# An attention maximum over the partitions, folded on VectorE and spread by two matmuls, in place of ten TensorE transposes

## The chip, the core and the metric

The kernel runs on one core of a Trainium2 chip. Its engines are named as in the profile: PE is TensorE (PEld its weight loads), DVE VectorE, ACT ScalarE, POOL GpSimd, and SP the engine that issues nearly all transfers. The metric is the time of one launch on the device, in microseconds (us); the median of several runs counts. [...]

## What is computed

Attention with queries averaged in pairs, and then a feed-forward layer that takes the largest of three products:

```
q_pool = q.reshape(B, H, S // 2, 2, D).mean(axis=3)          # 8 batches, 8 heads, 576 rows, 64 columns
scores = scale * (q_pool @ k^T)                              # 576 x 1152 a head
scores = scores - max(scores, axis=-1)
attn = exp(scores); attn = attn / (sum(attn, axis=-1) + 1e-9)
x = (attn @ v), heads side by side                           # 4608 x 512
h = max(x @ w1, x @ w2, x @ w3)                              # 4608 x 768
out = h @ w_out                                              # 4608 x 512
```

All is float32 to the outside. Inside, large products are split into a high and a low part in fp32r, a float32 of reduced precision, and summed.

## The kernel before

A **unit** is half the queries (288) of one pair of heads: 8 batches x 4 pairs x 2 halves = 64 units, numbered d = 0 to 63. The keys of a head, 1152, make nine blocks of 128. For each block `kk`, PE computes the scores of both heads transposed, keys on the partitions and 2 x 288 = 576 query columns along the free axis (`pqk`, L538 and L539, four matmuls of 288 columns). ACT copies them to SBUF (`s`, L544), and DVE keeps the running maximum over the blocks (`acc`, 128 x 576, L550 for the first and L553 for the seven others). The nine PSUM results share two buffers: a buffer comes free when its copy and its maximum are done.

After the ninth block `acc` holds, for each query column, 128 candidates, one a partition. The maximum over the partitions is taken in two pieces, of 3 x 115 = 345 columns (h = 0) and of 231 (h = 1). For a piece, PE transposes 116 columns at a time against the identity into PSUM (`pmt`, L589: three transposes, then two), DVE reduces each transposed block along its free axis to one value a query (`m`, L595), and PE transposes the values, broadcast to 128 columns, back over all partitions (`pmb`, L605: three, then two). These are the ten transposes of a unit. DVE then subtracts `pmb` from the scores (L620, three blocks by one piece at a time: 3 x 345 or 3 x 231 columns), ACT takes the exponential (L626), POOL sums over the nine blocks (`ksum`, L639 and L641, one addition of 576 columns each), and PE multiplies by the values (`pav`, L669, 36 matmuls in float32). The row sums go through PE (`psum`), a reciprocal on DVE (`rs`, L690; a column form of 96 x 6 in the first 16 units) and a scaling on POOL or DVE.

Beside that, the feed-forward runs in chunks of mostly 512 tokens, one batch behind the attention: `ph` (L931), `hm` (L952), `po` (L986). In the first third, DVE, ACT and POOL also unpack the feed-forward weights from 64-bit words (`w`, L831 to L864).

The order of all this is set when the program is built. Each piece of work is a `Step` with its engines, an assumed cost, the steps it comes after, and an urgency: the unit's number plus an entry of `RANK` for its kind, plus one of `NUDGE` for its name. `arrange` takes, at each turn, the engine that is free first, and gives it the most urgent step that is ready; where a step names two engines, the first that takes it has it. The result is a fixed list for each engine, and each engine then works through its list strictly in order and waits at the head for what an entry needs. Three dependences matter here. The first maximum of a unit (`kk == 1`) overwrites `acc`, which has one buffer, and so waits for the transposes of the unit before (`old.rows`). The PSUM pools `ps_a` and `ps_b` have one bank each, and hold `pmt`, `pmb` and, in `ps_b` from unit 8 on, `pav`, one after the other. And `pmb` of a unit may be written only after the subtractions of the unit before.

Of the kernel before, what the change touches and what calls it, by code (L numbers as in the profile page):

```python
# [18 lines left out]
P = 128  # L19
# [3 lines left out]
QH = 288  # L23
CB = 115
# [12 lines left out]
    "qk": -94.8622,  # L37
    "cp": -198.877,
    "mx": -110.1936,
    "rows": -297.5399,  # L40
    "red": -97.7108,
    "bc": -69.2978,
    "sub": 36.0255,
    "exp": -154.9623,
    "keys": -14.5562,
    "av": 14.8431,
    "xcopy": -242.7422,
    "psum": 306.6745,
    "eps": 163.4791,
    "inv": 411.5164,  # L50
    "xm": -165.8669,
    "load": 11.9358,
    "prep": 513.6605,
    "move": 372.9744,
    "split": 31.5471,
    "ffn": -33.8173,
    "rate": 1.0394,
    "mm": 49.1178,
    "fetch": -156.7626,
    "evac": -234.7904,  # L60
    "hhigh": 172.1589,
    "hlow": -152.0307,
    "conv": 478.2091,
    "rate0": 4.4379,
    "first_qk": 87.3127,
    "first_cp": -260.4178,
    "first_mx": 25.0784,
    "first_sub": 35.563,
    "first_exp": 326.0935,
    "first_keys": -44.827,  # L70
    "first_av": 37.0199,
    "first_xcopy": -183.8483,
    "first_psum": -32.0782,
    "first_inv": -61.85,
    "first_xm": -117.3451,
    "first_load": -320.6766,
    "first_prep": -184.3904,
    "first_move": -506.8185,
    "first_split": 49.1161,
# [991 lines left out]
```

## Time and profile before

| | |
|---|---|
| median of 3 runs | 1482.36 us (1482.32 to 1483.36) |
| span of the profiled execution, first to last instruction | 1480.9 us |
| TensorE clock granted, mean | 0.975 |
| PE busy with `ph`, `pav`, `pqk`, `po` on the chain that ended last | 27%, 13%, 14%, 10% of the span |
| PE busy with `pmt` and `pmb` on that chain | 2% and 2% |

The page gives no time for the profiled execution but its span. A busy time is the time in which an engine had an instruction at work; matmuls are pipelined, so their durations overlap, and PE's pace is read from one start to the next. "A <- B" in a list of waits says that A sat idle until B was done, with the sum in us, how often, and the longest. Groups of instructions are given as line, engine, operation, output <- inputs, shapes and count, then busy time and mean ns of one, and the idle time before them.

### The profile page before, as it was taken

Reading aid. Unit: us, or ns where it says so; the run is one execution under the profiler, and the core shown is the slowest. Engines: PE = TensorE matmul, PEld = TensorE weight load, DVE = VectorE, ACT = ScalarE, POOL = GpSimd, SP = SyncE. Lnnn points to the kernel's source line nnn. Section 1 sums busy time; section 2 is a strip of 40 time slices with the busy share of each in tenths; the row PEclk is TensorE's granted clock in tenths of the full one; section 3 lists DMA queues with packets and bytes.
Section 4 is the critical chain, followed back from the end, with each engine's and each line's share of the span. In section 5 each row is a group of like instructions: output and inputs, shape, how many; then the busy total and the mean of one; then the engine's idle time right before and its main releaser. Section 6 shows DMA issues by size and latency. Waiting matters only on the chain.

```text
span 1480.9 us, 24740 instructions
## 1 busy us (share of the span) xinstructions
PE 1400.6 (95%) x8704; PEld 1098.3 (74%) x8704; DVE 1046.1 (71%) x1441; ACT 904.5 (61%) x1464; POOL 1078.7 (73%) x835
## 2 busy tenths in 40 slices
PE   4788999888899999999999999999999999999999
PEld 4566666666567878778777777777777777778999
DVE  4898788989896875577777777877777778761110
ACT  4767766647676766467666676676766766651211
POOL 1888977686887868478887898789878988772210
PEclk9989899988999999999999999999999999999999
DMA  6556446657545665465566656664666556424441
GB/s 184 154 160 187 115 132 181 185 176 229 158 120 158 195 190 170 130 196 169 155 184 180 182 142 177 181 190 139 176 180 187 150 165 184 139 72 157 152 159 60
DMA packets 114762, 240.71 MB, mean 163 GB/s; under 512 B 15440, under 2 KB 75216, under 8 KB 114640
## 3 DMA queue, kind: packets, MB, share of 16 engines
q1 hardware_dynamic: 114064, 238.55, 55.2%
q8 instruction: 70, 1.15, 0.3%
q10 hardware_dynamic: 576, 0.59, 0.2%
q14 instruction: 52, 0.43, 0.1%
HBM read 144.70 MB, written 18.87 MB: 110 GB/s over the span
## 4 chain that ended last, share of the span: by engine, by line
PE 70%; DVE 4%; DMA 2%; issue 1%; POOL 1%; ACT 1%; SPq 0%; ACTq 0%; DVEq 0%
PE ph L931 27%; PE pav L669 13%; PE po L986 10%; PE pqk L538 7%; PE pqk L539 7%; PE pmt L589 2%; PE psum L683 2%; PE pmb L605 2%; DVE acc L553 1%; DMA w<-in_wout_dram 1%; DVE s L620 1%; DMA qq<-qraw 1%; POOL ksum L641 0%; DVE w L834 0%; DVE w L839 0%
## 5 line engine op out<-in xcount | busy, mean ns | idle before, releaser
L641 POOL TENSOR_TENSOR ksum<-ksum,s 128x576 f32<-128x576 f32 x448 | 638.0, 1424 | 28.9 <-ACT s L626 5.8
L931 PE MATMUL ph<-xh,w 128*128 128x512 f32 (+2 forms) x1440 | 464.6, 377 | 5.4 <-DVE hm L952 4.0
L620 DVE TENSOR_TENSOR s<-s,pmb 128x1035 f32<-128x1035 f32 (+1 forms) x384 | 396.9, 1049 | 46.0 <-PE pmb L605 46.0
L544 ACT COPY s<-pqk 128x576 f32<-128x576 f32 x576 | 362.5, 638 | 105.2 <-PE pqk L539 101.4
L538 PE MATMUL pqk<-qq,kc 128*128 128x288 f32 x1152 | 360.0, 327 | 57.1 <-DVE acc L553 35.3
L553 DVE TENSOR_TENSOR acc<-acc,pqk 128x576 f32<-128x576 f32 x448 | 335.3, 748 | 84.5 <-ACT s L544 81.7
L626 ACT ACTIVATE s<-s 128x1035 f32<-128x1035 f32 (+1 forms) x384 | 354.8, 934 | 60.2 <-DVE s L620 57.1
L539 PE MATMUL pqk<-qq,kc 128*128 128x288 f32 x1152 | 333.4, 304 | 0.0
L538 PEld LDWEIGHTS pqk<-qq,kc 128*128 128x128 f32 x1152 | 225.5, 196 | 113.5 <-DVE acc L553 51.7
L669 PE MATMUL pav<-s,v 128*64 128x288 f32 x2304 | 306.8, 419 | 1.8 <-DVE xr L724 1.4
L931 PEld LDWEIGHTS ph<-xh,w 128*128 128x128 f32 x1440 | 263.1, 188 | 45.9 <-DVE hm L952 4.9
L931 PE MATMUL ph<-xl,w 128*128 128x512 f32 (+2 forms) x720 | 268.4, 373 | 0.0
L669 PEld LDWEIGHTS pav<-s,v 128*64 128x64 f32 x2304 | 165.1, 141 | 122.0 <-issue 17.7
L539 PEld LDWEIGHTS pqk<-qq,kc 128*128 128x128 f32 x1152 | 227.9, 198 | 11.2
L962 POOL TENSOR_TENSOR h_lo<-hm,h_hi 128x512 fp32r<-128x512 f32 (+2 forms) x60 | 70.8, 1179 | 149.5 <-ACT h_hi L959 149.5
L639 POOL TENSOR_TENSOR ksum<-s 128x576 f32<-128x576 f32 x64 | 91.9, 1436 | 105.5 <-ACT s L626 103.1
L952 DVE TENSOR_TENSOR hm<-hm,ph 128x512 f32<-128x512 f32 (+2 forms) x120 | 75.4, 628 | 127.5 <-PE ph L931 127.5
L931 PEld LDWEIGHTS ph<-xl,w 128*128 128x128 f32 x720 | 135.8, 189 | 11.8
L595 DVE TENSOR_REDUCE m<-pmt 116x3 f32<-116x384 f32 (+1 forms) x128 | 61.1, 488 | 91.9 <-PE pmt L589 91.9
L434 POOL TENSOR_TENSOR kraw<-kraw 128x1152 fp32r<-128x1152 f32 x31 | 82.9, 2675 | 57.1 <-ACT kraw L430 39.4
L690 DVE RECIPROCAL rs<-rs 128x288 f32<-128x288 f32 (+1 forms) x64 | 96.3, 1506 | 18.5 <-ACT rs L687 18.2
L678 ACT COPY xr<-pav 128x288 f32<-128x288 f32 x64 | 25.4, 398 | 114.8 <-PE pav L669 114.6
(57 smaller groups left out, 1288.9 us busy)
## 6 DMA issues: line engine op xcount, KB each, us to landing
w<-w_split SPq DMA_DIRECT2D x144, 512.0 KB, 3.4
kc<-kraw SPq DMA_DIRECT2D x384, 96.0 KB, 2.3
qq<-qraw SPq DMA_DIRECT2D x252, 144.0 KB, 3.1
v<-in_vr_dram SPq DMA_DIRECT2D x32, 576.0 KB, 3.9
kraw<-in_kT_dram SPq DMA_DIRECT2D x31, 576.0 KB, 4.7
qraw<-in_qT_dram SPq DMA_DIRECT2D x31, 576.0 KB, 4.3
w<-in_win_dram SPq DMA_DIRECT2D x18, 512.0 KB, 4.8
w_split<-w SPq DMA_DIRECT2D x18, 512.0 KB, 4.9
```

Of the source, the lines that this page charges most:

```text
L538: nc.tensor.matmul(ps[:, h - hs[0], :QH], w, qq[:, 0, h], start=True, stop=False)
L539: nc.tensor.matmul(ps[:, h - hs[0], :QH], w, qq[:, 1, h], start=False, stop=True)
L544: nc.scalar.copy(o.s[kk // 3][:, kk % 3, slice(*hs)], o.ps[kk, hs][:, :, :QH])
L553: nc.vector.tensor_tensor(acc, acc, ps, op=ALU.max)
L620: nc.vector.tensor_tensor(s, s, o.pb[h][:, None, :w].broadcast_to([P, 3, w]), op=ALU.subtract)
L626: nc.scalar.activation(s, s, AF.Exp, scale=SCALE)
L639: vec[e].tensor_tensor(o.ksum, o.s[0][:, 0], x, op=ALU.add)
L641: vec[e].tensor_tensor(o.ksum, o.ksum, x, op=ALU.add)
L669: nc.tensor.matmul(o.pav[64 * h : 64 * h + 64, :QH], pr.v[:, kk, h], o.s[kk // 3][:, kk % 3, h], start=(kk == 0), stop=(kk == NK - 1),)
L690: nc.vector.reciprocal(o.rs, o.rs)
L931: nc.tensor.matmul(t.ps[:, : hi - lo], w[:, a, kk], xx[:, kk, lo:hi], start=(kk == 0 and i == 0), stop=(kk == 3 and i == 2),)
L986: nc.tensor.matmul(t.ps[:, : hi - lo], ww[:, kk, ms], hh[:, kk, lo:hi], start=(kk == 0 and i == 0), stop=(kk == 5 and i == 2),)
```

## The change

The maximum over the partitions is taken without PE. `fold` is one DVE reduce that reads `acc` in 32 x 32 blocks, transposes each and takes the maximum along the free axis: its result, 128 x 18, holds in each quarter of 32 partitions the maximum over these 32 keys, with query column 32 t + p at partition p, column t. `shift` copies the three upper quarters beside the first (three copies of 32 x 18), and `summit` reduces the four to one (`m`, 32 x 18). `m_high` and `m_low` split that value into an fp32r part and its remainder, on partitions 0 to 31 and 32 to 63 of `ml`. `spread_out` multiplies `ml` with a stacked pair of 32 x 32 identities (`pick`): 64 rows of 576 columns with the values on the diagonals, in one of two buffers `diag0` and `diag1` whose lower half was zeroed once. It may run on DVE or on POOL. Two matmuls of ones (`wide`, 128 x 128) against the halves of `diag`, 288 columns each, then leave the maximum of each column on all 128 partitions (`pmb`).

The pieces are now the two heads, 288 columns each, and subtraction and exponential follow that cut. The first maximum of a unit waits for the fold of the unit before instead of its transposes, and both stand on DVE. `ps_a` and `ps_b` no longer hold `pmt`. The tables `RANK` and `NUDGE` have new entries throughout, so that the order changes everywhere. An SBUF reserve for transfers that POOL would issue (it issues none here) is set to 1024 bytes.

```diff
-CB = 115
+SQ = 32
+NB = 18
...
 RANK = {
-    "qk": -94.8622,
+    "qk": -367.121,
...
 NUDGE = {
-    "av.0": -22.83, "av.1": -51.39, "av.10": -3.73, "av.11": -25.99, "av.12": 22.67, "av.13": 75.61,
+    "av.0": -107.82, "av.1": -655.65, "av.10": 832.07, "av.11": 458.97, "av.12": 42.87, "av.13": -71.19,
...
+    wide = cpool.tile([P, P], F32R, name="wide")
+    nc.vector.memset(wide.bitcast(F32), 1.0)
+    pick = cpool.tile([2 * SQ, SQ], F32, name="pick")
+    for i in range(2):
+        rows = slice(SQ * i, SQ * i + SQ)
+        nc.vector.tensor_copy(pick[rows], ident[rows, rows])
+    diag = [cpool.tile([P, NB, SQ], F32R, name=f"diag{i}") for i in range(2)]
+    for t in diag:
+        nc.vector.memset(t.bitcast(F32), 0.0)
...
-                    after = [c] + ([copies[0]] + (old.rows if old else []) if kk == 1 else [tops[-1]])
+                    after = [c] + ([copies[0]] + ([old.red] if old else []) if kk == 1 else [tops[-1]])
...
-        for h, (x0, x1) in enumerate([(0, 3 * CB), (3 * CB, 2 * QH)]):
-            nb, w = 3 - h, x1 - x0
-
-            def rows(e, h=h, nb=nb, x0=x0):
-                o.pt[h] = pools[h].tile([P, 512], F32, tag="ab"[h], name=f"pmt{d}_{h}")
-                acc = o.acc.rearrange("p h q -> p (h q)")[:, x0:]
-                for i in range(nb):
-                    nc.tensor.transpose(
-                        o.pt[h][: CB + 1, i * P : (i + 1) * P], acc[:, CB * i : CB * i + CB + 1], ident
...
+        def fold(e):
+            o.tops = small.tile([P, 4, NB], F32, tag="tops", name=f"tops{d}")
+            nc.vector.tensor_reduce(
+                o.tops[:, 0],
+                o.acc.rearrange("p h q -> p (h q)").rearrange("p (t k) -> p t k", t=NB),
+                axis=AX.X,
+                op=ALU.max,
+                apply_transpose=True,
+            )
+
+        def shift(e):
+            for g in range(1, 4):
+                nc.vector.tensor_copy(o.tops[:SQ, g], o.tops[SQ * g : SQ * g + SQ, 0])
+
+        def summit(e):
+            o.m = small.tile([SQ, NB], F32, tag="m", name=f"m{d}")
+            nc.vector.tensor_reduce(o.m, o.tops[:SQ].rearrange("p g t -> p t g"), axis=AX.X, op=ALU.max)
+
+        def m_high(e):
+            o.ml = small.tile([2 * SQ, NB], F32R, tag="ml", name=f"ml{d}")
+            nc.vector.tensor_copy(o.ml[:SQ], o.m)
+
+        def m_low(e):
+            nc.vector.tensor_tensor(o.ml[SQ:], o.m, o.ml[:SQ], op=ALU.subtract)
+
+        def spread_out(e):
+            vec[e].tensor_tensor(
+                diag[d % 2][: 2 * SQ],
+                pick[:, None, :].broadcast_to([2 * SQ, NB, SQ]),
+                o.ml[:, :, None].broadcast_to([2 * SQ, NB, SQ]),
+                op=ALU.mult,
+            )
+
+        o.red = step("red", d, [("dve", 0.667)], fold, [tops[-1]])
+        x = step("shift", d, [("dve", 0.24)], shift, [o.red])
+        x = step("top", d, [("dve", 0.142)], summit, [x])
+        y = step("top", d, [("dve", 0.085)], m_high, [x])
+        x = step("top", d, [("dve", 0.085)], m_low, [y])
+        full = step("diag", d, [dve(2 * QH), pool(2 * QH)], spread_out, [x] + (old2.bcs if old2 else []))
+        o.bcs = []
+        for h in range(2):
...
-            x = step("rows", d + 0.1 * h, [pe(133 * nb)], rows, [tops[-1], gone] + (old.subs[h] if old else []))
-            o.rows.append(x)
-            x = step("red", d, [("dve", 0.067 + nb * 0.133)], reduce, [x])
-            b = step("bc", d + 0.1 * h, [pe(89 + 99 * nb)], bcast, [x])
+            b = step("bc", d + 0.1 * h, [pe(133)], bcast, [full, gone] + (old.subs[h] if old else []), cols=QH)
...
-    nc = bacc.Bacc("TRN2", target_bir_lowering=False, num_devices=1)
+    nc = bacc.Bacc("TRN2", target_bir_lowering=False, num_devices=1, dynamic_dma_scratch_size=1024)
```

In the new order the diagonal is made by POOL in 20 units (3, 6, 8, 10, 13, 14, 18, 22, 24, 28, 30, 32, 36, 38, 42, 46, 48, 50, 52 and 59) and by DVE in the other 44. Two places show how the lists changed. A number behind a name's letters is the unit (`acc37` is unit 37's running maximum, `pqk38_0` the first score tile of unit 38, `s37_0` the first three score blocks of unit 37); what follows a last underscore tells buffers apart.

On DVE, at the end of unit 37's running maximum, before the change:

```order
L553 TENSOR_TENSOR acc37_7621<-acc37_7621,pqk37_7_7723 128x576
L690 RECIPROCAL rs35_7738<-rs35_7738 128x288
L553 TENSOR_TENSOR acc37_7621<-acc37_7621,pqk37_8_7733 128x576
L595 TENSOR_REDUCE m37_0_7785<-pmt37_0_7774 116x3
L595 TENSOR_REDUCE m37_1_7797<-pmt37_1_7787 116x2
L620 TENSOR_TENSOR s37_0_7599<-s37_0_7599,pmb37_0_7799 128x3x345
L550 TENSOR_TENSOR acc38_7819<-s38_0_7790,pqk38_1_7792 128x576
```

And at the same place after it:

```order
L578 TENSOR_TENSOR acc37_7444<-acc37_7444,pqk37_8_7564 128x576
L610 TENSOR_REDUCE tops37_7616<-acc37_7444 128x18
L737 RECIPROCAL rs35_7614<-rs35_7614 128x288
L620 COPY tops37_7616<-tops37_7616 32x18 x3
L624 TENSOR_REDUCE m37_7625<-tops37_7616 32x18
L628 CAST ml37_7627<-m37_7625 32x18
L631 TENSOR_TENSOR ml37_7627<-m37_7625,ml37_7627 32x18
L634 TENSOR_TENSOR diag1_109<-pick_105,ml37_7627 64x576
L667 TENSOR_TENSOR s37_0_7408<-s37_0_7408,pmb37_0_7639 128x3x288
L575 TENSOR_TENSOR acc38_7659<-s38_0_7637,pqk38_1_7631 128x576
```

Two reduces that each waited for PE are now a row of eight DVE instructions, with a reciprocal of unit 35 in their midst, and the first subtraction stands behind all of them.

On PE, from the product of unit 36 with its values (`pav36`, of which the last row is shown) to the spread of unit 37's maximum, before the change:

```order
L669 MATMUL pav36_7742<-s36_2_7498,v18_7174 64x288 x6
L589 MATMUL pmt37_0_7774<-ident_94,acc37_7621 116x128 x3
L538 MATMUL pqk38_0_7779<-qq19_0_7531,kc19_0_7425 128x288
L539 MATMUL pqk38_0_7779<-qq19_0_7531,kc19_0_7425 128x288
L538 MATMUL pqk38_0_7779<-qq19_0_7531,kc19_0_7425 128x288
L539 MATMUL pqk38_0_7779<-qq19_0_7531,kc19_0_7425 128x288
L589 MATMUL pmt37_1_7787<-ident_94,acc37_7621 116x128 x2
L538 MATMUL pqk38_1_7792<-qq19_0_7531,kc19_0_7425 128x288
L539 MATMUL pqk38_1_7792<-qq19_0_7531,kc19_0_7425 128x288
L538 MATMUL pqk38_1_7792<-qq19_0_7531,kc19_0_7425 128x288
L539 MATMUL pqk38_1_7792<-qq19_0_7531,kc19_0_7425 128x288
L605 MATMUL pmb37_0_7799<-ident_94,m37_0_7785 128x116 x3
```

And after it:

```order
L716 MATMUL pav36_7594<-s36_2_7353,v18_6964 64x288 x6
L563 MATMUL pqk38_1_7631<-qq19_0_7400,kc19_0_7226 128x288
L564 MATMUL pqk38_1_7631<-qq19_0_7400,kc19_0_7226 128x288
L563 MATMUL pqk38_1_7631<-qq19_0_7400,kc19_0_7226 128x288
L564 MATMUL pqk38_1_7631<-qq19_0_7400,kc19_0_7226 128x288
L652 MATMUL pmb37_0_7639<-diag1_109,wide_103 128x288
L978 MATMUL ph3_2_2_0_7574<-xh_116,w3_8_7453 128x512
L978 MATMUL ph3_2_2_0_7574<-xl_117,w3_8_7453 128x512
L978 MATMUL ph3_2_2_0_7574<-xh_116,w3_8_7453 128x512
L652 MATMUL pmb37_1_7649<-diag1_109,wide_103 128x288
L563 MATMUL pqk38_2_7651<-qq19_0_7400,kc19_0_7226 128x288
```

The transposes are gone, the first score tile of unit 38 now stands ahead of `pav36` (as do three `ph` matmuls behind the last scores of unit 37), and one matmul a piece is left of the spread.

More of the change, by code (lines that the diff above doesn't have):

```diff
@@ L36 @@
 RANK = {
-    "qk": -94.8622,
[L38 to L79, printed above, removed]
+    "qk": -367.121,
+    "cp": -157.85,
+    "mx": -372.477,
+    "red": -424.5991,
+    "shift": 218.3036,
+    "top": 471.3296,
+    "diag": -168.3272,
+    "bc": -652.2135,
+    "sub": 755.1676,
+    "exp": -77.4348,
+    "keys": 484.2481,
+    "av": -155.8274,
+    "xcopy": -495.8442,
+    "psum": 574.5454,
+    "eps": 154.6528,
+    "inv": -26.1003,
+    "xm": -523.4844,
+    "load": -101.8997,
+    "prep": 1286.9188,
+    "move": 398.6518,
+    "split": 200.0963,
+    "ffn": 230.3769,
+    "rate": -0.5905,
+    "mm": 112.971,
+    "fetch": -118.1147,
+    "evac": -754.3044,
+    "hhigh": -198.253,
+    "hlow": -705.5998,
+    "conv": 858.8277,
+    "rate0": 7.3554,
+    "first_qk": -785.226,
+    "first_cp": -585.909,
+    "first_mx": -200.8558,
+    "first_sub": 791.5253,
+    "first_exp": 611.1097,
+    "first_keys": -255.5291,
+    "first_av": -768.3727,
+    "first_xcopy": 8.2676,
+    "first_psum": -145.466,
+    "first_inv": -141.066,
+    "first_xm": 75.1779,
+    "first_load": 150.9309,
+    "first_prep": 256.4223,
+    "first_move": -487.1256,
+    "first_split": 381.6855,
 }
 NUDGE = {
[77 rows of a table removed]
[90 rows of a table added]
 }
@@ L577, in scores @@
                     uses.append([c, x])
-        o.rows, o.subs, o.exps, o.pt, o.pb, o.m = [], [[], []], {}, {}, {}, {}
+        o.subs, o.exps, o.pb = [[], []], {}, {}
         pools = (ps_a, ps_b)
-        for h, (x0, x1) in enumerate([(0, 3 * CB), (3 * CB, 2 * QH)]):
-            nb, w = 3 - h, x1 - x0
-            def rows(e, h=h, nb=nb, x0=x0):
-                o.pt[h] = pools[h].tile([P, 512], F32, tag="ab"[h], name=f"pmt{d}_{h}")
-                acc = o.acc.rearrange("p h q -> p (h q)")[:, x0:]
-                for i in range(nb):
-                    nc.tensor.transpose(
-                        o.pt[h][: CB + 1, i * P : (i + 1) * P], acc[:, CB * i : CB * i + CB + 1], ident
-                    )
-            def reduce(e, h=h, nb=nb):
-                o.m[h] = small.tile([CB + 1, 3], F32, tag=f"m{h}", name=f"m{d}_{h}")
-                nc.vector.tensor_reduce(
-                    o.m[h][:, :nb],
-                    o.pt[h][: CB + 1, : nb * P].rearrange("p (t k) -> p t k", t=nb),
-                    axis=AX.X,
-                    op=ALU.max,
-                )
-            def bcast(e, h=h, nb=nb):
-                o.pb[h] = pools[h].tile([P, 512], F32, tag="ab"[h], name=f"pmb{d}_{h}")
-                for i in range(nb):
-                    nc.tensor.transpose(
-                        o.pb[h][:, CB * i : CB * i + CB + 1],
-                        o.m[h][:, i : i + 1].broadcast_to([CB + 1, P]),
-                        ident[: CB + 1, : CB + 1],
-                    )
-            gone = xout[d - 1] if d > SPLIT and h else None
-            x = step("rows", d + 0.1 * h, [pe(133 * nb)], rows, [tops[-1], gone] + (old.subs[h] if old else []))
-            o.rows.append(x)
-            x = step("red", d, [("dve", 0.067 + nb * 0.133)], reduce, [x])
-            b = step("bc", d + 0.1 * h, [pe(89 + 99 * nb)], bcast, [x])
-            for i in range(3):
-                def sub(e, i=i, h=h, x0=x0, x1=x1, w=w):
-                    s = o.s[i].rearrange("p k h q -> p k (h q)")[:, :, x0:x1]
-                    nc.vector.tensor_tensor(
-                        s, s, o.pb[h][:, None, :w].broadcast_to([P, 3, w]), op=ALU.subtract
-                    )
-                def exp(e, i=i, x0=x0, x1=x1):
-                    s = o.s[i].rearrange("p k h q -> p k (h q)")[:, :, x0:x1]
@@ new lines, in scores, with bcast, sub, exp @@
+        o.red = step("red", d, [("dve", 0.667)], fold, [tops[-1]])
[6 more added lines that the diff above has]
+        for h in range(2):
+            def bcast(e, h=h):
+                o.pb[h] = pools[h].tile([P, 512], F32, tag="ab"[h], name=f"pmb{d}_{h}")
+                nc.tensor.matmul(
+                    o.pb[h][:, :QH],
+                    wide,
+                    diag[d % 2][:, NB // 2 * h : NB // 2 * h + NB // 2].rearrange("p t k -> p (t k)"),
+                    start=True,
+                    stop=True,
+                )
+            gone = xout[d - 1] if d > SPLIT and h else None
+            b = step("bc", d + 0.1 * h, [pe(133)], bcast, [full, gone] + (old.subs[h] if old else []), cols=QH)
+            o.bcs.append(b)
+            for i in range(3):
+                def sub(e, i=i, h=h):
+                    s = o.s[i][:, :, h]
+                    nc.vector.tensor_tensor(
+                        s, s, o.pb[h][:, None, :QH].broadcast_to([P, 3, QH]), op=ALU.subtract
+                    )
+                def exp(e, i=i, h=h):
+                    s = o.s[i][:, :, h]
@@ L626, in exp @@
                     nc.scalar.activation(s, s, AF.Exp, scale=SCALE)
                 r = d + 0.1 * i + 0.05 * h
-                x = step("sub", r, [dve(3 * w)], sub, [b, copies[-1]])
+                x = step("sub", r, [dve(3 * QH)], sub, [b, copies[-1]])
                 o.subs[h].append(x)
-                o.exps[i, h] = step("exp", r, [("act", 0.109 + w / 400)], exp, [x])
+                o.exps[i, h] = step("exp", r, [("act", 0.109 + QH / 400)], exp, [x])
         o.sums = []
```

165 rows, old and new, of the table NUDGE are left out of this document.

## The prediction

> **What bounds the kernel now.** I read the busy times first, then the span in stretches, then who waits for whom in each stretch, and last the order of time around one maximum.
>
> ```profile
> span 1480.9 us, 24740 instructions
> PE 1400.6 (95%) x8704; PEld 1098.3 (74%) x8704; DVE 1046.1 (71%) x1441; ACT 904.5 (61%) x1464; POOL 1078.7 (73%) x835
> ```
>
> ```profile
> 40.00:420.00 380.00, 325.91 (x2133) 237.18 (x2132) 326.42 (x547) 257.98 (x420) 305.11 (x227) 0.91 0.58 167
> 420.00:1327.00 907.00, 903.27 (x5545) 703.61 (x5545) 679.09 (x831) 599.59 (x956) 729.42 (x563) 1.00 0.57 165
> 1327.00:1481.00 154.00, 150.56 (x952) 141.17 (x950) 22.73 (x39) 29.29 (x64) 34.92 (x36) 1.00 0.38 129
> ```
>
> The columns are the length, the busy time of PE, PEld, DVE, ACT and POOL with counts, the granted clock and the DMA share. There are three regimes. From 40 to 420 us PE is busy for 326 of 380 us at a granted clock of 0.91, and DVE for as long: 86% each. From 420 to 1327 us PE is busy for 903 of 907 us at full clock, DVE for 75% and POOL for 80%. The last 154 us are feed-forward matmuls with nothing else beside them. The waits inside the first two stretches (PE's and DVE's for 40 to 420, then the same for 420 to 1327) say which of the two engines leads:
>
> ```profile
> PE pqk L538 <- DVE acc L553: 29.9, 37, 2.9
> DVE acc L553 <- ACT s L544: 22.7, 22, 5.8
> DVE m L595 <- PE pmt L589: 8.1, 11, 1.7
> ...
> PE pmt L589 <- ACT xr L678: 3.0, 4, 0.9
> PE pmb L605 <- DVE m L595: 0.7, 1, 0.7
> DVE m L595 <- PE pmt L589: 82.6, 67, 3.1
> DVE s L620 <- PE pmb L605: 44.9, 40, 3.7
> ```
>
> In the first stretch PE waits 29.9 us for DVE's running maximum: DVE leads. In the second PE waits 3.7 us in all, and DVE waits 127.5 us for the ten transposes (82.6 + 44.9): PE leads, and a microsecond taken from its queue there is a microsecond off the end, if nothing new makes it wait.
>
> **What PE loses and gains.** PE's order of time around the maximum of unit 37 (start, duration, line):
>
> ```profile
> 805.69 0.54 PE L589 MATMUL pmt<-ident,acc 128*116 128x128 f32 x3
> 805.98 0.38 PE L538 MATMUL pqk<-qq,kc 128*128 128x288 f32 x1
> 806.20 0.30 PE L539 MATMUL pqk<-qq,kc 128*128 128x288 f32 x1
> 806.33 0.29 PE L538 MATMUL pqk<-qq,kc 128*128 128x288 f32 x1
> 806.46 0.30 PE L539 MATMUL pqk<-qq,kc 128*128 128x288 f32 x1
> 806.60 0.38 PE L589 MATMUL pmt<-ident,acc 128*116 128x128 f32 x2
> 806.73 0.38 PE L538 MATMUL pqk<-qq,kc 128*128 128x288 f32 x1
> 806.95 0.29 PE L539 MATMUL pqk<-qq,kc 128*128 128x288 f32 x1
> ...
> 807.34 0.46 PE L605 MATMUL pmb<-ident,m 116*128 116x116 f32 x3
> 807.57 0.39 PE L538 MATMUL pqk<-qq,kc 128*128 128x288 f32 x1
> 807.80 0.29 PE L539 MATMUL pqk<-qq,kc 128*128 128x288 f32 x1
> ...
> 808.20 0.36 PE L605 MATMUL pmb<-ident,m 116*128 116x116 f32 x2
> 808.33 0.48 PE L931 MATMUL ph<-xh,w 128*128 128x512 f32 x1
> 808.64 0.40 PE L931 MATMUL ph<-xl,w 128*128 128x512 f32 x1
> 808.88 0.63 PE L931 MATMUL ph<-xh,w 128*128 128x512 f32 x2
> ```
>
> Matmuls overlap, so I count from start to start. The four groups of transposes hold the queue for 0.29, 0.13, 0.23 and 0.13 us: 0.78 us. The matmul behind a group also comes late: 0.22 us to the next start at 805.98, 806.73 and 807.57, where a score matmul otherwise takes 0.13 (806.20 to 806.33), and 0.31 against 0.24 at 808.33: 0.34 us more. Ten transposes cost 1.12 us a unit.
>
> What comes is two matmuls of 288 columns on fp32r operands, as the score matmuls are: 0.13 us each, without the late start, since their neighbours are of the same kind. One late start stays, as the scores now follow the f32 product `pav` directly. New cost 0.35 us; net 0.77 us a unit. The number of units in the second stretch is the count of the row of first maxima in it:
>
> ```profile
> L550 DVE TENSOR_TENSOR acc<-s,pqk 128x576 f32<-128x576 f32 x44 | 33.0, 750 | 10.2 <-ACT s L544 6.3 <-PE pmt L589 3.7
> ```
>
> 44 units of 20.6 us (907 / 44): 44 x 0.77 = **34 us less**. The other 20 units lie in the first stretch, where PE doesn't lead.
>
> **What DVE gains.** The rows of the operations that go, and the nearest to those that come (mean ns behind the bar):
>
> ```profile
> L595 DVE TENSOR_REDUCE m<-pmt 116x3 f32<-116x384 f32 x64 | 35.5, 555 | 81.2 <-PE pmt L589 81.1
> L595 DVE TENSOR_REDUCE m<-pmt 116x2 f32<-116x256 f32 x64 | 26.9, 420 | 10.7 <-PE pmt L589 10.7
> L620 DVE TENSOR_TENSOR s<-s,pmb 128x1035 f32<-128x1035 f32 x192 | 235.2, 1229 | 45.4 <-PE pmb L605 45.4
> L620 DVE TENSOR_TENSOR s<-s,pmb 128x693 f32<-128x693 f32 x192 | 166.6, 870 | 0.5 <-PE pmb L605 0.5
> L690 DVE RECIPROCAL rs<-rs 128x288 f32<-128x288 f32 x48 | 93.5, 1948 | 18.2 <-ACT rs L687 18.2
> L690 DVE RECIPROCAL rs<-rs 96x6 f32<-96x6 f32 x16 | 2.8, 181 | 0.3
> L710 DVE TENSOR_SCALAR rs<-psum 96x6 f32<-96x6 f32 x16 | 2.4, 152 | 2.3 <-PE psum L700 2.3
> L641 POOL TENSOR_TENSOR ksum<-ksum,s 128x576 f32<-128x576 f32 x448 | 638.0, 1424 | 28.9 <-ACT s L626 5.8
> L420 DVE TENSOR_TENSOR qraw<-qraw 128x288 f32<-128x288 f32 x2 | 0.9, 454 | 3.1 <-DMA qraw<-in_qT_dram 3.1
> ```
>
> Two reduces go: 0.975 us a unit. A reduce costs 1.05 ns a column (555 - 420 over 128 columns), so the fold over 576 columns takes 0.757 us if the transposing adds nothing, and the maximum over 72 takes 0.226. Three copies, the cast and the remainder, 18 columns wide, lie between 0.152 and 0.181 each: 5 x 0.17 = 0.85. The diagonal over 576 columns is 0.75 (the row of first maxima) on DVE, where 44 units have it, or 1.42 on POOL for 20. Together +1.61 us of DVE a unit with the diagonal, +0.86 without: on average +1.38, 88 us in all. The subtractions keep their columns (1035 + 693 before, 864 + 864 now), so they cost the same. The constants set up once (two zeroed diagonals, the ones) are some 1300 columns, about 1.4 us at a nanosecond a column; they stand ahead of the first sum of q, which waited 3.1 us for its load, and cost nothing. No transfer comes or goes: SP has 526 rows in both orders, and POOL issues none.
>
> The fold is an operation that no row shows. Below it stands the plain reduce; far above, the reciprocal row, 6.2 ns a column, would make it 3.7 us. I take the reduce, whose operation it is. A second pass over the columns would add 0.6 us a unit. [...]
>
> In the second stretch DVE goes from 15.4 us a unit (679 / 44) to 16.8 of the new 19.8, and POOL from 16.6 to 17.0: both stay below PE, so I hide them behind PE's queue there, except 4 us for chains that come late (rival 2). In the first stretch DVE leads: 19 units x 1.38 = 26 us more work, less the 9 us at most for which it waited there for transposes; its 54 us of idle time can take some. Between -5 (all hidden, some of PE's 15 us shows) and +26 I take +13.
>
> Sum: 1480.9 - 34 + 4 + 13 = 1464 for a profiled span. The median of the runs, 1482.36, is 1.5 above the span, which is what lies around it: **1465 us**, by itself 1450 to 1478.
>
> **Rivals.**
>
> 1. *DVE and POOL collide.* Of the new DVE instructions, the four copies and casts read and write SBUF alone, and the remainder and the diagonal read two SBUF tensors. If such an instruction has to wait for POOL's running one, each waits half of 1.42 us, four times in five (POOL's 80%): 0.57 us, six times 3.4, about 3.2 us a unit with the diagonals that POOL makes itself. It decides from about 3 us a unit: DVE's 16.8 then pass PE's 19.8. The second stretch would then run at some 21.2 us a unit (DVE 20.0, and 1.2 of waits that its strict order can't fill), 26 us longer than before; the first gets 19 x (1.38 + 3.2) = 87 us of DVE work against 27 us that its idle time could take: 60 longer. 1482 + 86 = **1568 us**, and up to 1700 if each waits for a whole POOL instruction. For it: in all of the program before, DVE has no two-input SBUF instruction beside a busy POOL. Against it: the sixteen 96x6 reciprocals, SBUF to SBUF, kept 0.181 us while POOL was at work. [...]
> 2. *The chain becomes the bound.* Before, PE needed one short reduce between its two groups. Now eight DVE instructions, one after the other, stand before the spread. [...] Whatever makes the spread wait holds unit 38's scores and the feed-forward matmuls behind it on PE, and on DVE the subtractions. If PE loses 0.4 us a unit more, and the first stretch the full 26: 1482 - 34 + 18 + 26 = **1492 us**.
> 3. *The first stretch gains too.* The new order fills DVE's idle time there, and PE's 15 us show in part, with the clock of 0.91 a little higher: 1482 - 34 - 10 = **1438 us**.
>
> **Chances.** The forecast 0.40, rival 1 0.34, rival 2 0.18, rival 3 0.08. A measurement of this kernel tells a change from none by about 0.2%, 3 us. Faster: 0.40 + 0.08 + 0.02 of rival 2, 0.50. Same: 0.09, from rival 2. Slower: 0.34 + 0.07, 0.41. As both signs hold much, the range goes from 1436, rival 3, to 1610, which leaves out the worst third of rival 1.
>
> **What would show it.** PE's start-to-start time of the two spreading matmuls (0.13 each) and of the score matmul behind them (0.13, not 0.22); the fold's mean ns (757; far more says the transposing costs); the copies' mean ns, where 150 to 180 denies rival 1 and 500 or more proves it, as would POOL instructions above 1.46 us; PE's waits for DVE between 420 and 1327 us, 3.7 us before, where more than 20 is rival 2; the date at which PE becomes dense, 420 us before, 433 forecast. What would make me wrong most: rival 1, whose price no row of before can tell.

## The result, and the profile after

The changed kernel takes 1634.82 us (median of 4 runs, 1632.75 to 1635.81) against 1482.48 for the kernel before: a ratio of 1.1026, 95% interval 1.1011 to 1.1041. It is slower by 152 us; the forecast was 1465. The profiled run has a span of 1632.1 us.

The page's busy times first, then the stretches of before (length, then busy time and count of PE, PEld, DVE, ACT and POOL, granted clock, DMA share, GB/s):

```profile
PE 1422.0 (87%) x8192; PEld 1109.4 (68%) x8192; DVE 1304.4 (80%) x1810; ACT 904.1 (55%) x1464; POOL 1109.1 (68%) x855
```

```profile
40.00:420.00 380.00, 304.74 (x1826) 225.20 (x1826) 343.49 (x556) 224.75 (x353) 275.24 (x197) 0.84 0.50 146
420.00:1327.00 907.00, 810.87 (x4564) 623.73 (x4560) 775.21 (x995) 539.87 (x873) 676.84 (x526) 0.93 0.52 152
```

PE is no longer dense in the second stretch: 811 of 907 us instead of 903, at a granted clock of 0.93 instead of 1.00. In the first it is busy for 305 us instead of 326, at 0.84 instead of 0.91, and DVE for 343 instead of 326. Through all runs below the clock of the second stretch goes, by and large, with PE's busy time there, from 0.92 at 796 us to 1.00 at 902; what the lower clock costs by itself was not tested. DVE's busy time rises by 258 us (1046.1 to 1304.4), where the new work was put at 88. The groups by line say where the rest is (mean ns of one behind the bar):

```profile
L620 DVE COPY tops<-tops 32x18 f32<-32x18 f32 x192 | 133.4, 695 | 3.8
L634 DVE TENSOR_TENSOR diag<-pick,ml 64x576 fp32r<-64x576 f32 x44 | 52.0, 1182 | 1.4
L610 DVE TRANSPOSE_TENSOR_REDUCE tops<-acc 128x18 f32<-128x576 f32 x64 | 49.3, 770 | 1.5
L628 DVE CAST ml<-m 32x18 fp32r<-32x18 f32 x64 | 40.9, 639 | 1.9
L631 DVE TENSOR_TENSOR ml<-m,ml 32x18 fp32r<-32x18 f32 x64 | 29.1, 455 | 2.2
L624 DVE TENSOR_REDUCE m<-tops 32x18 f32<-32x72 f32 x64 | 16.5, 258 | 1.7
```

The fold costs what was forecast, and the last reduce (258 ns, forecast 226) nearly so. Four of the six do not: a copy of 18 columns takes 695 ns, though the shortest of them took 164, and the cast 639 against a shortest of 154. Their idle time before is nearly nothing, so the waiting is counted inside the instruction. Counted from the shortest times of the four groups (164, 154, 167 and 743 ns), the excess is 192 x 0.531 + 64 x 0.485 + 64 x 0.288 + 44 x 0.439 = 102 + 31 + 18 + 19 = **170 us**. What they wait for is seen in the order of time around one maximum (start, duration, engine, line; of DVE, POOL and PE):

```profile
991.97 0.79 POOL L740 TENSOR_TENSOR xr<-xr,rs 128x288 f32<-128x288 f32 x1 [2.09 <-DVE m L624]
992.00 0.78 DVE L628 CAST ml<-m 32x18 fp32r<-32x18 f32 x1
992.72 1.40 POOL L688 TENSOR_TENSOR ksum<-ksum,s 128x576 f32<-128x576 f32 x1
992.82 1.32 DVE L631 TENSOR_TENSOR ml<-m,ml 32x18 fp32r<-32x18 f32 x1
994.07 2.61 POOL L459 TENSOR_TENSOR kraw<-kraw 128x1152 fp32r<-128x1152 f32 x1
994.18 3.11 DVE L634 TENSOR_TENSOR diag<-pick,ml 64x576 fp32r<-64x576 f32 x1
997.34 0.61 PE L652 MATMUL pmb<-diag,wide 128*128 128x288 f32 x1 [5.40 <-DVE diag L634]
```

The cast ends at 992.78, 0.02 us behind POOL's `xr` (992.76). The remainder ends at 994.14, 0.02 behind POOL's `ksum` (994.12). The diagonal ends at 997.29, 0.61 behind POOL's `kraw` (996.68), which is about its own work. Each hangs on an instruction of an engine whose data it doesn't use, and PE, behind it, stands still for 5.4 us. The whole trace says the same. Of these 364 instructions 163 took over 60 ns more than the shortest of their kind; all 163 began while POOL was at work, and ended 0.02 to 0.03 us behind the end of a POOL instruction (one copy 0.09, the diagonals 0.61). Of the other 201, four began while POOL was at work, in the last 0.2 us of its instruction.

Where the loss lies is read from the dates of two first maxima, those of units 20 and 63, in before and after (the date stands behind the three durations):

```profile
L550 DVE TENSOR_TENSOR acc<-s,pqk x1: 747/747/747, 422.7 to 422.7; 128x576 f32<-128x576 f32 x1
...
L550 DVE TENSOR_TENSOR acc<-s,pqk x1: 745/745/745, 1302.8 to 1302.8; 128x576 f32<-128x576 f32 x1
```

```profile
L575 DVE TENSOR_TENSOR acc<-s,pqk x1: 747/747/747, 485.3 to 485.3; 128x576 f32<-128x576 f32 x1
...
L575 DVE TENSOR_TENSOR acc<-s,pqk x1: 754/754/754, 1469.1 to 1469.1; 128x576 f32<-128x576 f32 x1
```

Units 0 to 19 take 62.6 us longer (485.3 - 422.7). The next 43 take 983.8 instead of 880.1, 22.88 us each instead of 20.47: 103.7 longer. The rest up to the span's end is 15.1 shorter (163.0 instead of 178.1), because the new order starts feed-forward work earlier: 897 `ph` and `po` matmuls start behind that date instead of 969. Sum: +151.2.

### The profile page after: what moved, and what is told of

Its sections match the earlier page's. It is cut to its first block, busy times and chain, and to the rows that moved or that the text cites. A ratio compares the mean times of both kernels' runs of the same rounds, so it can differ in the third digit from the quotient of the medians.

```text
span 1632.1 us, 23935 instructions
## 1 busy us (share of the span) xinstructions
PE 1422.0 (87%) x8192; PEld 1109.4 (68%) x8192; DVE 1304.4 (80%) x1810; ACT 904.1 (55%) x1464; POOL 1109.1 (68%) x855
## 4 chain that ended last, share of the span: by engine, by line
PE 51%; DVE 33%; issue 7%; ACT 4%; DMA 2%; POOL 2%; SPq 1%; ACTq 0%; DVEq 0%; POOLq 0%
PE ph L978 20%; PE pav L716 9%; DVE tops L620 7%; PE po L1033 7%; DVE acc L578 6%; PE pqk L563 6%; PE pqk L564 5%; DVE s L667 3%; DVE diag L634 2%; DVE tops L610 2%; DVE rs L737 2%; DVE ml L628 2%; ACT s L569 2%; DVE ml L631 1%; PE pmb L652 1%
## 5 line engine op out<-in xcount | busy, mean ns | idle before, releaser
L688 POOL TENSOR_TENSOR ksum<-ksum,s 128x576 f32<-128x576 f32 x448 | 642.1, 1434 | 31.1 <-ACT s L673 10.3
L978 PE MATMUL ph<-xh,w 128*128 128x512 f32 (+2 forms) x1440 | 470.4, 382 | 5.0 <-DVE xr L771 2.6
L563 PE MATMUL pqk<-qq,kc 128*128 128x288 f32 x1152 | 369.4, 335 | 81.3 <-DVE acc L578 35.3
L673 ACT ACTIVATE s<-s 128x864 f32<-128x864 f32 x384 | 352.9, 929 | 107.8 <-DVE s L667 106.2
L667 DVE TENSOR_TENSOR s<-s,pmb 128x864 f32<-128x864 f32 x384 | 393.6, 1045 | 15.3 <-PE pmb L652 15.1
L564 PE MATMUL pqk<-qq,kc 128*128 128x288 f32 x1152 | 348.0, 316 | 0.0
L563 PEld LDWEIGHTS pqk<-qq,kc 128*128 128x128 f32 x1152 | 239.5, 208 | 153.3 <-DVE acc L578 46.2
L978 PEld LDWEIGHTS ph<-xh,w 128*128 128x128 f32 x1440 | 271.2, 194 | 46.1 <-DVE xr L771 2.8
L978 PE MATMUL ph<-xl,w 128*128 128x512 f32 (+2 forms) x720 | 274.4, 381 | 0.0
L564 PEld LDWEIGHTS pqk<-qq,kc 128*128 128x128 f32 x1152 | 241.5, 210 | 12.4
L999 DVE TENSOR_TENSOR hm<-hm,ph 128x512 f32<-128x512 f32 (+2 forms) x120 | 75.5, 629 | 104.5 <-PE ph L978 103.7
L652 PE MATMUL pmb<-diag,wide 128*128 128x288 f32 x128 | 43.6, 397 | 112.2 <-DVE diag L634 106.6
L620 DVE COPY tops<-tops 32x18 f32<-32x18 f32 x192 | 133.4, 695 | 3.8
L652 PEld LDWEIGHTS pmb<-diag,wide 128*128 128x128 f32 x128 | 26.7, 232 | 132.3 <-DVE diag L634 121.4
```

What stands on the lines that cost most here:

```text
L563: nc.tensor.matmul(ps[:, h - hs[0], :QH], w, qq[:, 0, h], start=True, stop=False)
L564: nc.tensor.matmul(ps[:, h - hs[0], :QH], w, qq[:, 1, h], start=False, stop=True)
L620: nc.vector.tensor_copy(o.tops[:SQ, g], o.tops[SQ * g : SQ * g + SQ, 0])
L667: nc.vector.tensor_tensor(s, s, o.pb[h][:, None, :QH].broadcast_to([P, 3, QH]), op=ALU.subtract)
L673: nc.scalar.activation(s, s, AF.Exp, scale=SCALE)
L688: vec[e].tensor_tensor(o.ksum, o.ksum, x, op=ALU.add)
```

## The experiments

Three theories stood at the start. **Lock**: a DVE instruction that copies from SBUF to SBUF, or reads two operands in SBUF, waits until POOL's running instruction ends. **Chain**: eight DVE instructions in a row before the spread cost this, whatever each waits for. **Order**: the new table of priorities costs it, not the operations. Every run keeps the changed kernel's order of work, but for the instructions that its edit names.

**Copies and cast written as reduces.**

```
-                nc.vector.tensor_copy(o.tops[:SQ, g], o.tops[SQ * g : SQ * g + SQ, 0])
+                nc.vector.tensor_reduce(o.tops[:SQ, g], o.tops[SQ * g : SQ * g + SQ, 0, :, None], axis=AX.X, op=ALU.max)
...
-            nc.vector.tensor_copy(o.ml[:SQ], o.m)
+            nc.vector.tensor_reduce(o.ml[:SQ], o.m[:, :, None], axis=AX.X, op=ALU.max)
```

> The three shift copies and the cast are written as a tensor_reduce over an axis of one element, as the summit's reduce (258 ns mean in the changed kernel) did not seem to wait for POOL; the remainder and the diagonal keep their two SBUF inputs, and the order of work is the same. Lock theory (a DVE copy or two-SBUF-input instruction waits until POOL's running instruction ends): the moved 32x18 instructions fall from 695 and 639 ns mean to 160 to 200, the remainder (455 ns) rises, since the cast no longer waits just ahead of it; about 133 us of DVE's 1304 go, and at 0.6 us of time per us of DVE (152 us of time for 258 us of DVE) the time comes to about 1560 us (1530 to 1590). Chain theory (eight instructions in a row before the spread, whatever each waits for) and order theory (the new priorities are what costs): 1625 to 1640 us.

Measured: 1513.83 us, ratio to before 1.0222 (1.0193 to 1.0251). Groups of this run:

```profile
L634 DVE TENSOR_TENSOR diag<-pick,ml 64x576 fp32r<-64x576 f32 x44 | 58.6, 1332 | 1.4
L631 DVE TENSOR_TENSOR ml<-m,ml 32x18 fp32r<-32x18 f32 x64 | 56.7, 886 | 2.2
...
L620 DVE TENSOR_REDUCE tops<-tops 32x18 f32<-32x18 f32 x192 | 30.9, 161 | 3.9
...
L628 DVE TENSOR_REDUCE ml<-m 32x18 fp32r<-32x18 f32 x64 | 10.1, 158 | 1.9
```

The same bytes moved between the same places take 161 ns instead of 695 once the operation is another; the remainder, now without a wait just ahead of it, rises from 455 to 886, as expected. Chain and order theories, both of which had put this run at 1625 us or more, fall, since neither the number of instructions nor their sequence has changed. My time was 46 us too high: DVE lost 101 us of busy time and the kernel 121 us, so 0.6 us per us was too low a price.

**An operand in PSUM for every new instruction.** The spare columns of one PSUM bank hold the fold's output, the maximum and the remainder; the fp32r part (`mh`) stays in SBUF. The bank also takes the spread of the first head, so the trace calls that `pa`. All 64 diagonals are DVE's here, 20 more than in the changed kernel:

```
+    pa = ps_a.tile([P, 512], F32, tag="a", name="pa")
...
-            o.tops = small.tile([P, 4, NB], F32, tag="tops", name=f"tops{d}")
+            o.tops = pa[:, QH : QH + 4 * NB].rearrange("p (g t) -> p g t", g=4)
...
-            o.m = small.tile([SQ, NB], F32, tag="m", name=f"m{d}")
+            o.ml = pa[: 2 * SQ, 360 : 360 + NB]
+            o.m = o.ml[:SQ]
...
+            o.mh = small.tile([SQ, NB], F32R, tag="ml", name=f"mh{d}")
+            nc.vector.tensor_copy(o.mh, o.m)
...
-            nc.vector.tensor_tensor(o.ml[SQ:], o.m, o.ml[:SQ], op=ALU.subtract)
+            nc.vector.tensor_tensor(o.ml[SQ:], o.m, o.mh, op=ALU.subtract)
...
-            vec[e].tensor_tensor(
+            nc.vector.tensor_tensor(
```

> [...] Lock theory: no group of them above 300 ns (diagonal 0.75 to 0.80 us), DVE's busy time 1304 less 170 of waits, plus 15 for 20 more diagonals, about 1150 us; the time 1465 us (1445 to 1495), the forecast without the collision. Chain theory: 1490 and above, PE's wait for the diagonal still 100 us. Order theory: 1550 and above though the instructions are short.

Measured: 1465.20 us, ratio 0.9894 (0.9875 to 0.9912): faster than before by 1%, and the forecast's 1465. Groups, and then the dates of units 20 and 63:

```profile
L636 DVE TENSOR_TENSOR diag<-pick,pa 64x576 fp32r<-64x576 f32 x64 | 47.4, 741 | 1.2
L621 DVE COPY pa<-pa 32x18 f32<-32x18 f32 x192 | 34.5, 180 | 6.5
...
L633 DVE TENSOR_TENSOR pa<-pa,mh 32x18 f32<-32x18 f32 x64 | 11.3, 177 | 2.1
L630 DVE CAST mh<-pa 32x18 fp32r<-32x18 f32 x64 | 10.5, 163 | 1.8
```

```profile
L576 DVE TENSOR_TENSOR acc<-s,pqk x1: 746/746/746, 436.0 to 436.0; 128x576 f32<-128x576 f32 x1
...
L576 DVE TENSOR_TENSOR acc<-s,pqk x1: 753/753/753, 1302.7 to 1302.7; 128x576 f32<-128x576 f32 x1
```

No wait is left in any of them, with chain and order as they were: 164 of the 192 copies began while POOL was at work, and none took more than 185 ns. The run on the diagonals' engine, below, is the control for the 20 that POOL no longer makes. The first 20 units are 13.3 us later than before (436.0 - 422.7), 43 units take 866.7 (20.16 each) instead of 880.1, and the rest 161.7 instead of 178.1.

**The three copies in SBUF, the rest as in that run.** The lines on `tops` are the changed kernel's again.

> As the run with everything in PSUM, but fold, copies and summit's input stay in SBUF, so only the three copies a unit can collide with POOL. Lock theory: copies stay at 500 to 750 ns mean (192 of them, some 100 us above 164 ns each), cast, remainder and diagonal are short; the time lies between the changed kernel and the run with all in PSUM, by DVE's waits 102 of 170 parts of the way from it: about 1565 us. If the copies' waits are harmless because the cast would have waited instead, it lies within 20 us of the run with all in PSUM. Chain and order theories: no nearer to 1482 than that run.

Measured: 1564.72 us, ratio 1.0568 (1.0514 to 1.0621).

```profile
L621 DVE COPY tops<-tops 32x18 f32<-32x18 f32 x192 | 142.6, 742 | 3.8
```

The copies alone are worth 99.5 us of the 169.6 between the changed kernel and the run without waits; they take 192 x (0.742 - 0.180) = 108 us longer than there.

**All diagonals on DVE**, in the changed kernel, the control for the engine of 20 of them: `vec[e]` in line 634 becomes `nc.vector`.

> Only the engine of 20 of the 64 diagonals changes, from POOL to DVE: the control for the two runs with PSUM. Lock theory: DVE gains 20 x 1.18 = 24 us, POOL loses 23 us of 1109, so each collision is a little rarer: 1635 us within 15. If the diagonals on POOL (1.15 us each, behind its queue) were a main cost, 1600 or less.

Measured: 1668.22 us, ratio 1.1273 (1.1223 to 1.1323): 33 us more, outside my 15. DVE's busy time rises by 26 us (1304.4 to 1330.3), more than half of it in the copies:

```profile
L620 DVE COPY tops<-tops 32x18 f32<-32x18 f32 x192 | 151.0, 787 | 3.8
```

That POOL's work falls by 25 us did not make collisions rarer. The two PSUM runs thus won in spite of this edit.

**The same copies, off the chain.** To the run without waits, three SBUF copies a unit of a scratch tile nobody reads are added behind the diagonal:

```
+            for g in range(1, 4):
+                nc.vector.tensor_copy(junk[:SQ, g], junk[SQ * g : SQ * g + SQ, 0])
```

> The run with everything in PSUM (1465.2 us) gets three more copies a unit, 32x18 from SBUF to SBUF, of a scratch tile that nobody reads, right behind the diagonal on DVE: as many colliding copies as the run with the three shift copies in SBUF (1564.7 us), but none of them in the chain that leads to the spread of their own unit. The copies should take 500 to 750 ns each, DVE's busy time about 1146 + 192 x 0.65 = 1270 us. If the loss comes from DVE's time alone (throughput): about 1565 us, as where they stand in the chain. If it comes from the chain being longer while PE stands before the spread (latency): DVE leads the first 20 units, so some 34 us come there as before, and little in the other 44: 1495 to 1515 us.

Measured: 1565.87 us, ratio 1.0565 (1.0546 to 1.0584). Group, and dates of units 20 and 63:

```profile
L645 DVE COPY junk<-junk 32x18 f32<-32x18 f32 x192 | 119.2, 621 | 3.7
```

```profile
L578 DVE TENSOR_TENSOR acc<-s,pqk x1: 744/744/744, 468.5 to 468.5; 128x576 f32<-128x576 f32 x1
...
L578 DVE TENSOR_TENSOR acc<-s,pqk x1: 753/753/753, 1402.8 to 1402.8; 128x576 f32<-128x576 f32 x1
```

Throughput, not latency: 119 us of copies (88 of them waiting, by the shortest of 164 ns) that no spread of their unit waits for cost 101 us, in the first 20 units (468.5 - 436.0 = 32.5, 1.6 each) and in the other 43 (934.3 - 866.7 = 67.6, 1.6 each) alike. The second stretch has no room for them. Why, is in DVE's waits there. In the run without waits:

```profile
DVE acc L579 <- ACT s L570: 89.5, 64, 4.4
DVE s L669 <- PE pa L654: 21.5, 24, 3.4
```

In this one:

```profile
DVE acc L581 <- ACT s L572: 86.6, 68, 4.4
...
DVE s L673 <- PE pa L658: 1.0, 2, 0.7
```

The wait for ACT's copy of the scores, some 90 us or 2 us a unit, stays in every run with the new order (86.6 to 95.0), whether the clock was 0.92 or 1.00; in the kernel before it was 52.7. Only the wait for PE gives way, and of it the run without waits has 21.5 us for 45 units, half a microsecond each.

**POOL made quieter**, in the changed kernel: of each unit's eight additions, only the first and the last are made, so six of the nine blocks are missing from its sums.

```
-                else:
+                elif kk == NK - 1:
                     vec[e].tensor_tensor(o.ksum, o.ksum, x, op=ALU.add)
```

> The changed kernel with six of the eight additions of every unit's sum of keys left out on POOL (384 instructions of 1.43 us, 550 of POOL's 1109 us); DVE's instructions and all places of memory are as in the changed kernel. Lock theory: POOL is busy about 37% of the time instead of 68%, so the waits of copies, cast, remainder and diagonals fall to a half or less: copies 695 to 350 to 450 ns mean, and the time to about 1540 us (1500 to 1570). If something else slows these instructions (the place in memory, the partition shift, DMA writes), the copies stay at 600 to 750 ns, and the time at 1620 and above.

Measured: 1527.80 us, ratio 1.0312 (1.0270 to 1.0354). POOL is busy for 567.2 us of 1529.0, 37%, and

```profile
L620 DVE COPY tops<-tops 32x18 f32<-32x18 f32 x192 | 68.5, 357 | 3.8
```

Nothing on DVE was edited, and its copies halve. It is POOL that they wait for.

**Back to POOL with 20 diagonals**, and **without the remainder**, each from the run without waits. In the first, maximum and remainder are also kept in SBUF for the units whose diagonal is POOL's (`ml` is that copy); the second drops lines 628 and 631 and spreads from 32 rows.

```
+            ml = o.mlb if e == "pool" else o.ml
-            nc.vector.tensor_tensor(
+            vec[e].tensor_tensor(
```

> The run with everything in PSUM, but the 20 diagonals that the order gives to POOL are made there again, from maximum and remainder in SBUF; the other 44 as before in that run. DVE gets 20 x 0.74 = 15 us less, POOL some 23 us more, and those 20 chains wait for POOL's queue. If DVE's time counts: 1452 to 1462 us. If the wait behind POOL's additions counts (its idle time is 26% there): 1465 to 1480 us. In the changed kernel the same edit went from 1634.8 to 1668.2 us in the other direction, so by that 33 us less, 1432 us.

> The run with everything in PSUM without cast and remainder: the spread maximum is the maximum rounded as fp32r by the diagonal's own output, on 32 rows instead of 64; the quotient of the softmax doesn't change by a shift that is the same for all keys of a query. DVE gets 64 x 0.34 = 22 us less, the chain 0.4 us shorter. The first 20 units, which DVE leads, give 7 us, the others 0 to 3: 1456 us (1450 to 1462). If the chain no longer matters anywhere: 1463 to 1466 us.

Measured: 1459.43 us (ratio 0.9852, 0.9836 to 0.9868) and 1454.30 us (0.9816, 0.9794 to 0.9838), both within the range put down for DVE's time: 5.8 and 10.9 us below the run without waits, for 10.6 and 21.7 us less of DVE. The 33 us that the diagonals cost in the locked kernel are not to be had here.

**Both, and both with the shift on ACT.** In the second, `nc.vector.tensor_copy` of the shift becomes `nc.scalar.copy`.

> The two better versions in one: no cast and no remainder (the run without them: 1454.3 us, 10.9 below the run with everything in PSUM), and 20 diagonals back on POOL, from a maximum in SBUF there (the run with them: 1459.4 us, 5.8 below). If DVE's time is what the first 20 units and the margin of the others lack, both add up: 1448.5 us (1444 to 1453). If they free the same idle time: 1454 us.

> As the run with both, but the three shift copies a unit go from DVE to ACT, at the same place in the program. [...] If DVE's busy time counts alone: about 1430 us. If DVE's waits count as its work does (strict order): some 1 us lost for 0.54 saved a unit, 0.46 x 64 = 29 us more: 1478 us (1455 to 1490).

Measured: 1448.93 us (ratio **0.9788**, 0.9775 to 0.9802), and 1450.96 us (0.9797, 0.9783 to 0.9810). The gains add up, and PE is busy for 902 of the second stretch's 907 us again:

```profile
420.00:1327.00 907.00, 902.21 (x5389) 705.41 (x5386) 735.00 (x1006) 605.49 (x969) 758.90 (x587) 1.00 0.58 170
```

On ACT the copies bring nothing more: 33 us of DVE's work go (1113.0 to 1080.2) and 30 us of waits for ACT come: 21.6 in the units whose diagonal is DVE's, as shown, and 8.7 in the others:

```profile
L628 DVE TENSOR_REDUCE pa<-pa 32x18 f32<-32x72 f32 x44 | 9.6, 219 | 21.7 <-ACT pa L621 21.6
```

Both outcomes that I had put down for it (1430, 1478) were wrong, since each took one side of that account for nothing. The "some 1 us lost" a unit behind the second is shown by no run: the waits for ACT came to 30.3 us, 0.47 a unit.

## Why the prediction was wrong

- **The step that failed** is the price of the small DVE instructions: "Three copies, the cast and the remainder, 18 columns wide, lie between 0.152 and 0.181 each", and the diagonal at 0.75. On DVE beside a busy POOL they took 0.695, 0.639, 0.455 and 1.18. Freed of the wait, they took 0.180, 0.163, 0.177 and 0.741, so the work in them was priced right and 170 us of waiting was left out of the sum. That was rival 1, whose mean wait (0.57 us) also was near: 0.53 for the copies, 0.49 for the cast, 0.29 for the remainder, 0.44 for the diagonal. In part that was luck: not four in five waited but 163 of 364, and each of these waited 1.04 us on average, not 0.71. Which instructions would have to wait was a supposition there, which no row of before showed. The runs show it: copy, cast and the two with both inputs in SBUF waited (0.695, 0.639, 0.455 and 1.18), with an operand in PSUM they did not (0.180, 0.163, 0.177 and 0.741), and a reduce in place of the copy didn't (0.161).
- **What was held against rival 1** was no evidence: the 96x6 reciprocal, SBUF to SBUF, takes 0.176 us in the changed kernel as well, beside copies at 0.695. So that row says nothing of a copy.
- **Rival 1's own time, 1568,** was too low in one term, the room that DVE has beside PE. The first 20 units were put 60 us later and came 62.6 later. The second stretch was put at 21.2 us a unit, with 20.0 of DVE and 1.2 of waits that its order can't fill. It came at 22.88, with DVE busy for 775.21 of 907 us: 19.6 of work and 3.3 of idle time. The same sizing is behind "It decides from about 3 us a unit": the 170 us are 2.7 us a unit, less than that, and decided all the same. I took all of DVE's idle time for room, and some 2 us a unit of it is the wait for ACT's copies, which no run with the new order filled.
- **PE's saving** of 34 us, less 4 for late chains, was right in size, and hidden. In the run without waits everything behind unit 20 gains 13.4 + 16.4 = 29.8 us. The 16.4 behind unit 63 are about the 72 matmuls that start earlier (17 us at the 0.24 from one `ph` to the next). As 68 of them fall into the 43 units between, these save some 0.7 us each, where 0.77 was forecast. The spreading matmuls stand as forecast in its order of time (PE):

```profile
701.46 0.29 PE L565 MATMUL pqk<-qq,kc 128*128 128x288 f32 x1
701.59 0.29 PE L654 MATMUL pa<-diag,wide 128*128 128x288 f32 x1
701.72 0.29 PE L654 MATMUL pmb<-diag,wide 128*128 128x288 f32 x1
701.85 0.34 PE L564 MATMUL pqk<-qq,kc 128*128 128x288 f32 x1
```

  From start to start 0.13, 0.13 and 0.13 to the score matmul behind, not 0.22.
- **The first stretch**, +13, came at +13.3 in the same run. That it fits so closely is luck: 13 was chosen between -5 and +26, and the four runs with less work on DVE came at +0.9 to +10.4. The fold, put at 757 ns if the transposing adds nothing, came at 770.
- **Rival 2**, the chain as the bound, is not what happened: the chain cost what it did by the waits in it. A change of engine cost 0.03 to 0.08 us in the median in the trace before, by its waits (32 ns from ACT to DVE, 56 from DVE to PE, 79 from DVE to POOL). The 0.4 us a unit in its sum is shown by no run: PE's wait for the diagonal in the second stretch came to 63.9 us in the changed kernel, 1.6 a unit, and to 0.3 us in the run with the same chain and no collisions (us, times, longest):

```profile
PE pmb L652 <- DVE diag L634: 63.9, 22, 5.6
```

```profile
PE pa L654 <- DVE diag L636: 0.3, 1, 0.3
```

- Of the signs named, the copies' mean (500 or more) spoke for rival 1, and the runs showed it. The mean of POOL's additions stayed at 1434 ns, but six of the 448 took 1801 to 1935 ns, each begun under a diagonal of DVE; none took above 1466 before. So nearly all of the waiting, not all, lay on DVE's side. PE's waits for DVE in the second stretch passed the 20 us named for rival 2 (63.9 for the diagonal and 23.6 for the running maximum), but could not tell the two rivals apart, since the waiting instructions stand in that chain.

How 170 us of waits split into DVE's lost time and PE's later starts can't be read from one run. The copies cost 99.5 us for 108 more of DVE's time on the chain and 101 for 119 off it, so most is DVE's time. What the new order by itself gains or costs was not tested: no run has the old order with the new instructions.

## What to carry to other kernels

Before a small instruction is given to DVE, look at what POOL does meanwhile and where the operands lie: here a copy of 18 columns could cost a whole POOL instruction and more (5.38 us at the longest, against 0.164 at the shortest), and the profile then shows it as a long copy, not as idle time (133.4 us busy and 3.8 idle in the 192). An operand in PSUM, or a reduce over one element in place of a copy, took the wait away at nearly the same price (180 and 161 ns against 164). An engine's room is not its idle share but the part of its waits that gives way when it gets more work; here 0.5 us a unit instead of 3.

## What the runs showed of the hardware

One copy of 18 columns took 5.38 us, the longest of the changed kernel. In the order of time (DVE, then POOL) it is the first of a pair:

```profile
797.94 5.56 DVE L620 COPY tops<-tops 32x18 f32<-32x18 f32 x2
```

```profile
797.77 1.58 POOL L818 TENSOR_TENSOR xl<-xr,xh 128x32 fp32r<-128x32 f32 x3
799.31 1.41 POOL L688 TENSOR_TENSOR ksum<-ksum,s 128x576 f32<-128x576 f32 x1
800.68 2.61 POOL L459 TENSOR_TENSOR kraw<-kraw 128x1152 fp32r<-128x1152 f32 x1
```

It ends at 803.32 (797.94 + 5.38), 0.03 us behind `kraw` (803.29), though three `xl` and then `ksum`, at 800.72, had ended before: it waited through the ends of four POOL instructions, each followed by the next without a gap. That is the exception: 97 of the 104 copies that waited ended behind the first POOL instruction to end, seven only behind a later one. At 992 to 997 us, above, the waits ended with each instruction, though the next of POOL followed as closely; what decides between the two stays open. The prediction's half of one instruction was thus no upper bound. An operand in PSUM cost the copies 16 ns (180 against the shortest of 164 in SBUF), and the fold 22 ns when it wrote there (792 against 770).
